# Block means of V from whole tiles, sums carried by transfers, and a new list of priorities in a three-layer kernel

## The chip, the cores and the metric

The kernel runs on one core of a Trainium2 chip. The metric is device time in microseconds (us) of one execution. The engines are TensorE (PE in the rows; PEld is its weight load), VectorE (DVE), ScalarE (ACT), GpSimd (POOL) and SyncE (SP), which issues all the transfers (DMAs).

## The reference, cut to what matters

Three layers run one after another on 2 sequences of 768 positions, all in float32.

1. Attention with 8 heads of 64. A position sees its neighbours within 15 positions, and also one summary of each of the 24 blocks of 32 positions: the key's summary is the maximum over the block, the value's summary is the mean.

```
k_sum = k.reshape(B, H, nb, block, D).max(axis=3)
v_sum = v.reshape(B, H, nb, block, D).mean(axis=3)
```

2. A mixture of four causal attention heads, gated by the best two of four logits, with projections `wq`, `wk`, `wv`, `wo`.
3. A channel mix: `r * (relu(xk @ w_k)**2 @ w_v)` with `r = sigmoid(xr @ w_r)`. Its three weight matrices come as float64 and are turned into float32 pairs on the chip.

## The kernel before, in words

The sequence is cut into 12 tiles of 128 positions (`t` = 0 to 5 for the first batch element, 6 to 11 for the second) for layer 1, and into 4 chunks of 384 for layers 2 and 3. Products that need full precision are split into a high and a low part and take three matmuls.

**Layer 1, per tile.** `stage1_scores` runs 32 small matmuls (L627) of queries against a key slab that holds a window of 96 keys and 24 block summaries. `stage1_softmax` adds the mask and takes the row maximum on DVE (L642, 8 per tile), the exponential with its row sum on ACT (L645, 8 per tile), one sum and one reciprocal for each half of the heads (L648, L650), and a multiplication by the reciprocal (L653 or L657). The probabilities lie in `pp` buffers, of which there are four, two per tile. `stage1_trans` transposes them on TensorE (L680) and copies them out, and `stage1_out` multiplies them by the values (L698). The value buffer of a half tile (`vw`; for some tiles it borrows `oh`, `ol`, `pq0` to `pq2`) holds 96 window rows loaded from memory and 24 rows of block means, which `put_val_sums` copies in from `vs`, two copies of 24x512 for each of the tiles 0 to 7, on whichever of DVE, ACT and POOL the planner chooses.

**Block means of V.** For batch element 0, `val_sums0` multiplies all 12 value windows, as they lie in `vw`, by a small matrix `own` that has a load of its own (L557, 4 matmuls per window), and copies the result to `vs`. It therefore needs every window of the first element. The rows of `vw` that hold no window are set to zero first (L493). For element 1, `sums1` loads V in four pieces of 96x8x128, folds each with three additions on DVE or POOL (L578), multiplies it by a selection matrix (L582) and copies it out on ACT (L584).

**Layers 2 and 3.** Projections of queries and keys (L770) and of values and gates (L788), scores (L870), transposes (L930), weighted values (L956), the output projection (L998); then L1106, L1129 and L1153 for the channel mix. Their weights pass through the two `stage` buffers and are split into high and low parts by copies and subtractions (L409, L411, L416, L418). The weights of layer 2 are loaded by `load_w12` after the first five tiles of layer 1 have been written down.

**What sets the order.** The program is not run in the order in which it is written. Each operation is handed to a planner (`Plan`) with an estimated cost, and some with several engines to choose from. The planner simulates the engines with fixed delays between them. It takes the ready operation that can start first, and among equals the one with the highest priority; priority is the length of the chain of work behind an operation, plus a bias. It does so 100 times with random numbers added to the priorities, keeps the shortest result (L193 to L213), and issues the instructions of every engine in that order. Each engine then works through its own list in order. Loads that are written down while `first[0]` is "sp" form a chain and keep their order on the SP queue.

Of the kernel before, what the change touches and what calls it, by code (L numbers as in the profile page):

```python
# [19 lines left out]
E = 4  # L20
# [6 lines left out]
NV = S // 8  # L27
# [30 lines left out]
ORDERS, SPREAD = 100, 1000.0  # L58
# [10 lines left out]
class Buf:  # L69


    def __init__(self, pool, shape, dt, name):
        self.pool, self.shape, self.dt, self.name = pool, shape, dt, name
        self.tile, self.slot, self.left, self.first, self.last = None, None, 0, None, 0.0
        self.hist = []
# [11 lines left out]
class Plan:  # L87
# [14 lines left out]
        "sp": dict(pe=995.0, act=995.0, dve=995.0, pool=995.0, sp=995.0),  # L102
    }
    HOLD = dict(pe=200.0, act=225.0, dve=200.0, pool=135.0, sp=995.0)
# [4 lines left out]
    for a in MODES:  # L109
        for b in MODES:  # L110
            SWITCH[a, b] = 92.0
# [48 lines left out]
    def run(self, alloc):  # L160
# [28 lines left out]
        need = {o: o.need for o in self.ops}  # L189
        left = {b: b.left for b in sum(self.order.values(), [])}  # L190
        best = None
        rng = random.Random(1)
        for n in range(ORDERS):  # L193
            for o in self.ops:
                o.need = need[o]
                o.rank = o.prio + (rng.random() * SPREAD if n else 0.0)
                o.eng, o.cost, o.fn, o.lock = o.ways[0]
            for b in left:
                b.left, b.slot, b.last = left[b], None, 0.0
            done = self.simulate()  # L200
            if done is None:
                continue
            end = max(o.end for o in done)
            if best is None or end < best[0]:
                best = (end, [(o, o.start, o.eng, o.cost, o.fn, o.end) for o in done], {b: b.slot for b in left})
        for b in left:
            b.slot = best[2][b]
        for o, o.start, o.eng, o.cost, o.fn, o.end in best[1]:
# [4 lines left out]
        return best[0]  # L213

    def simulate(self):
# [5 lines left out]
        cols = {}  # L221
# [27 lines left out]
        while len(done) < len(self.ops):  # L249
            best = None  # L250
            for e, cand in ready.items():
                mine = None
                for o in cand:
# [10 lines left out]
                    for b in o.bufs:  # L264
                        if b.slot is None:
# [5 lines left out]
                            t = max(t, sorted(free[b.pool])[n][0])  # L271
                    rank = o.rank
# [14 lines left out]
            for b in o.bufs:  # L287
                if b.slot is None:
                    free[b.pool].sort()
                    b.slot = free[b.pool].pop(0)[1]  # L290
                    nxt[b.pool] += 1
# [11 lines left out]
            if e == "sp":  # L303
                clock["sp"] = t + 560.0
                bus = max(bus, t + 1100.0) + o.cost
                o.end = bus
            for b in o.bufs:
# [41 lines left out]
def dma(nbytes, run=512):  # L349
    return nbytes / 275.0 * (1 if run >= 512 else 1.5 if run >= 384 else 2)  # L350
# [3 lines left out]
def attn_moe_rwkv(  # L354
# [15 lines left out]
    owns: bass.AP,  # L370
# [8 lines left out]
    NSM, NSE = 8, 4  # L379
# [18 lines left out]
    def load(dst, src, nbytes, run=512, w=None):  # L398
        op("sp", dma(nbytes, run), lambda: nc.sync.dma_start(dst(), src), w=w, stream=first[0])
# [52 lines left out]
    cst = buf("cst", [P, P + NB + 16])  # L452
    own = buf("x2", [P, 4 * NB - 4])
# [6 lines left out]
    sms, rss = buf("sms", [P, NSM, 4, 2]), buf("rss", [P, NSM, 4])  # L460
# [31 lines left out]
    for t in range(TPB):  # L492
        op("pool", 700, lambda t=t: nc.gpsimd.memset(vw[t][0].t[SROW[0]], 0.0), w=[(vw[t][0], "sum")])  # L493
# [8 lines left out]
    def slab(t):  # L502
# [3 lines left out]
        if b:  # L506
            load(lambda: k.t[:, :, NB:NB + SLAB], kS[b, :, :, tt * P:tt * P + SLAB], P * HP * SLAB * 4, 640,
# [15 lines left out]
    def load_v(t, s2):  # L523
# [3 lines left out]
        load(lambda: v.t[WROW[s2]], vp[b, a:a + KS0], KS0 * 2048, w=[(v, "win")])  # L527
# [17 lines left out]
    def val_sums0():  # L545

        vsm[0] = vs = buf("vs", [P, DM])
        p = bank("a2")
        for t in range(TPB):
            for s2 in range(2):  # L550
                v = vw[t][s2]

                def go(t=t, s2=s2, v=v):
                    n = NK if s2 == 0 else KS0
# [794 lines left out]
```

## Time and profile before

| | us |
|---|---|
| three runs | 1180.05, 368.61, 367.28 |
| median of them | 368.61 |
| the profiled execution | 368.59 |
| its span, first to last instruction | 366.8 |
| TensorE busy | 347.4 (95%) |
| VectorE busy | 256.1 (70%) |
| ScalarE busy | 219.7 (60%) |
| GpSimd busy | 75.5 (21%) |

The profiled execution agrees with the median; 1.8 us of it lie outside the span. The granted TensorE clock is full in all 40 slices of the span. Busy shares are means over the whole span, and a matmul counts as busy while it is in the pipeline, so that two that overlap, or one that waits within it, hide how much work there was. The transfers are dense in the first tenth and thin afterwards: the engines that move them are busy for 80 to 90% in the first slices and for a tenth or less in most of the last twenty.

### The profile page before, as it was taken

Reading aid. Unit: us, or ns where it says so; the run is one execution under the profiler, and the core shown is the slowest. Engines: PE = TensorE matmul, PEld = TensorE weight load, DVE = VectorE, ACT = ScalarE, POOL = GpSimd, SP = SyncE. Lnnn points to the kernel's source line nnn. Section 1 sums busy time; section 2 is a strip of 40 time slices with the busy share of each in tenths; the row PEclk is TensorE's granted clock in tenths of the full one; section 3 lists DMA queues with packets and bytes.
Section 4 is the critical chain, followed back from the end, with each engine's and each line's share of the span. In section 5 each row is a group of like instructions: output and inputs, shape, how many; then the busy total and the mean of one; then the engine's idle time right before and its main releaser. Section 6 shows DMA issues by size and latency. Waiting matters only on the chain.

```text
span 366.8 us, 7505 instructions
## 1 busy us (share of the span) xinstructions
PE 347.4 (95%) x2768; PEld 297.9 (81%) x2768; DVE 256.1 (70%) x813; ACT 219.7 (60%) x612; POOL 75.5 (21%) x105
## 2 busy tenths in 40 slices
PE   1687999999999999999999999999999999999996
PEld 0566988777877899797978798889988998889986
DVE  2899989899999867999999969219640576003511
ACT  2889757899979568898888766035610454015400
POOL 3228402315271003713414301000100001000000
PEclk9999999999999999999999999999999999999999
DMA  8996546753413310113334100100001000100001
GB/s 268 254 320 172 180 120 180 178 184 96 144 46 116 115 59 1 60 57 116 116 114 118 57 1 9 50 29 2 0 29 59 1 0 2 57 29 2 0 29 59
DMA packets 18740, 31.42 MB, mean 86 GB/s; under 512 B 1936, under 2 KB 9104, under 8 KB 18704
## 3 DMA queue, kind: packets, MB, share of 16 engines
q1 hardware_dynamic: 18704, 30.94, 27.3%
q8 instruction: 22, 0.36, 0.4%
q14 instruction: 14, 0.11, 0.1%
HBM read 27.79 MB, written 3.15 MB: 84 GB/s over the span
## 4 chain that ended last, share of the span: by engine, by line
PE 78%; DVE 13%; DMA 7%; issue 1%; SPq 0%
PE ps L1153 18%; PE ps L1129 16%; PE ps L1106 8%; PE ps L770 8%; PE ps L788 5%; PE ps L930 5%; PE ps L870 4%; PE ps L998 4%; PE a L956 3%; DMA qb<-in_qT 3%; PE a L698 2%; DVE pp L642 2%; DMA stage<-in_vp 2%; DMA vw<-in_vp 1%; PE ps L680 1%; PE ps L627 1%
## 5 line engine op out<-in xcount | busy, mean ns | idle before, releaser
L645 ACT ACTIVATE pp<-pp,nm 128x120 f32<-128x120 f32 x96 | 36.6, 386 | 6.2 <-DVE nm L642 6.1
L408 ACT ACTIVATE pp<-ps 128x512 f32<-128x512 f32 x12 | 7.1, 590 | 49.6 <-PE ps L1106 49.6
L890 ACT ACTIVATE pq<-pq,nm 128x128 f32<-128x128 f32 (+5 forms) x48 | 31.8, 663 | 7.9 <-DVE nm L877 5.2
L1159 DVE TENSOR_TENSOR wvgl<-ps,pp 128x512 f32<-128x512 f32 (+1 forms) x13 | 8.5, 650 | 40.0 <-PE ps L1153 40.0
L770 PE MATMUL ps<-x,wqkh 128*128 128x384 f32 x128 | 34.3, 349 | 0.5 <-DVE q L416 0.5
L877 DVE CUSTOM_DVE_ANT_0 pq<-ps,trm 128x384 f32<-128x384 f32 (+3 forms) x64 | 29.2, 502 | 4.0 <-PE ps L870 3.9
L1136 DVE SCALAR_TENSOR_TENSOR q<-ps,q 128x384 f32<-128x384 f32 x32 | 17.6, 554 | 18.3 <-ACT q L1135 17.9
L930 PE MATMUL ps<-cst,pq 128*128 128x128 f32 x168 | 25.0, 275 | 0.1
L642 DVE CUSTOM_DVE_ANT_0 pp<-ps,msk 128x120 f32<-128x120 f32 x96 | 22.3, 272 | 3.8 <-PE ps L627 3.7
L416 DVE TENSOR_TENSOR x<-q,x 128x384 fp32r<-128x384 f32 x24 | 13.2, 567 | 16.3 <-ACT x L408 16.1
L418 POOL TENSOR_TENSOR x<-q,x 128x384 fp32r<-128x384 f32 x8 | 12.0, 1498 | 61.2 <-ACT x L408 61.1
L1135 ACT ACTIVATE q<-ps 128x384 f32<-128x384 f32 x32 | 15.6, 489 | 13.9 <-PE ps L1129 12.7
L770 PEld LDWEIGHTS ps<-x,wqkh 128*128 128x128 f32 x128 | 22.1, 189 | 1.5 <-DVE q L416 0.7
L788 PE MATMUL ps<-wvgh,x 128*128 128x260 f32 x96 | 23.1, 304 | 0.0
L627 PE MATMUL ps<-kw,qb 64*64 64x120 f32 x320 | 12.0, 296 | 10.9 <-DMA qb<-in_qT 7.6
L1129 PE MATMUL ps<-x,wqkh 128*128 128x384 f32 x96 | 21.9, 341 | 0.0
L770 PE MATMUL ps<-x,wqkl 128*128 128x384 f32 x64 | 21.5, 337 | 0.0
L930 PEld LDWEIGHTS ps<-cst,pq 128*128 128x128 f32 x168 | 19.5, 141 | 1.8 <-issue 0.3
L956 PE MATMUL a<-th,vv 128*64 128x384 f32 (+2 forms) x144 | 20.7, 423 | 0.0
L408 ACT ACTIVATE th<-ps 128x384 f32<-128x384 f32 x45 | 19.6, 493 | 1.4 <-PE ps L930 1.3
L870 PE MATMUL ps<-ks,q 64*128 64x384 f32 (+3 forms) x192 | 20.3, 339 | 0.0
L1089 DVE SCALAR_TENSOR_TENSOR q<-x,mu,q 128x384 f32<-128x384 f32 x32 | 19.3, 612 | 0.8 <-ACT q L427 0.8
(229 smaller groups left out, 969.9 us busy)
## 6 DMA issues: line engine op xcount, KB each, us to landing
stage<-in_wk SPq DMA_DIRECT2D x8, 512.0 KB, 3.6
stage<-in_wv SPq DMA_DIRECT2D x8, 512.0 KB, 3.6
qb<-in_qT SPq DMA_DIRECT2D x12, 256.0 KB, 5.8
vw<-in_vp SPq DMA_DIRECT2D x16, 192.0 KB, 3.4
out_y<-wvgl SPq DMA_DIRECT2D x11, 256.0 KB, 2.0
stage<-in_wr SPq DMA_DIRECT2D x4, 512.0 KB, 4.0
kw<-in_kS SPq DMA_DIRECT2D x6, 320.0 KB, 3.6
ks<-in_kS SPq DMA_DIRECT2D x4, 400.0 KB, 5.1
```

The costliest lines, as they stand in the source:

```text
L642: op("dve", dve(NK), lambda i=i, p=p: nc.vector.tensor_tensor_reduce(pr.t[:, i], p.t[:, i * NK:(i + 1) * NK], msk.t[:, m], -0.125, BIG, AL ...
L645: op("act", act(NK, True) + 186, lambda i=i: nc.scalar.activation(pr.t[:, i], pr.t[:, i], AF.Exp, bias=nm.t[:, i:i + 1], scale=-1.0, accum ...
L770: mm(p.t[:, :C], a.t[:, kc, cols], x.t[:, kc, :], start=(kc == 0 and i == 0), stop=(kc == KC - 1 and i == 2))
L788: mm(p.t[:, :260], x.t[:, kc, tok], a.t[:, kc, :], start=(kc == 0 and i == 0), stop=(kc == KC - 1 and i == 2))
L870: mm(ps[e2].t[:, :z - a], q1.t[r, x, tok], ks.t[r, y, a:z], start=n == 0, stop=n == 2)
L877: nc.vector.tensor_tensor_reduce(pr.t[:, a:z], p.t[:, :z - a], trm.t[:, 512 - nk + a:512 - nk + z] if z == nk and not a else (trm.t[:, 512 ...
L890: nc.scalar.activation(pr.t[:, :nk], pr.t[:, :nk], AF.Exp, bias=nm.t[:, m:m + 1], scale=-1.0, accum_out=sme.t[:, k, i, 0:1]), r=[nm, (sme, ...
L930: lambda i=i, kb=kb, pr=pr: nc.tensor.transpose(p.t[:, i * P:(i + 1) * P], pr.t[:, kb * P:(kb + 1) * P], ident()),
L956: mm(acc.t[64 * e2:64 * e2 + 64, tq0 * P:(tq0 + cnt) * P], vv.t[:, kb, e * D:(e + 1) * D], th[e2].t[:, i0 * P:(i0 + cnt) * P], start=first ...
L1106: mm(p.t, a.t[:, kc, tok], w[2](), start=(kc == 0 and i == 0), stop=(kc == KC - 1 and i == 2))
L1129: mm(p.t[:, :C], w[2]()[:, mo:mo + P], a.t[:, kc, :], start=(kc == 0 and i == 0), stop=(kc == KC - 1 and i == 2))
L1153: mm(p.t[:, :n], a[2]()[:, tok], w[2]()[:, col], start=(m == 0 and i == 0), stop=(m == FC - 1 and i == 2))
```

## The change: what it does

- **Means of element 0.** V is loaded a second time, as two whole tiles of 128x3x512 (`val_tiles`, 768 KB each) in buffers of the pool `x`, in the chain ahead of the windows. The matrix `own` is now part of `consts`, and 24 matmuls replace 48. The zeroing of `vw` and the load of `own` go.
- **Means of element 1.** Three loads of 128x2x512 in `stage`, 24 matmuls into one bank, four copies out. The twelve additions go.
- **Carrying the means.** For every tile but the first, the two copies into `vw` become two transfers of 24x512 (48 KB) on the SP queue. For tile 0 one copy is on DVE and one on ACT by preference.
- **Probabilities of tiles 0, 1 and 2** lie in the three `x2` buffers, not in `pp`.
- **One sum and one reciprocal per tile** over 8 columns in place of two over 4.
- **Loads.** Weights for values and gates are loaded after the windows of tile 0, those for queries and keys after the windows of tile 2, the queries of tiles 2 and 3 after the windows of tiles 0 and 1.
- **Planner.** The 100 random orders go; 161 listed seeds (`STEPS`) each shift the priorities of some operations, all are applied, and one simulation gives the order. Delays and costs of transfers and of some matmuls change, and at most eight transfers are taken to be in flight.

```diff
-ORDERS, SPREAD = 100, 1000.0
+STEPS = (
+    785053421, 541001281, 764893564, 565041234, 822100463, 391705521, 731851593, 744830411, 695749570, 1026508739,
...
-        "sp": dict(pe=995.0, act=995.0, dve=995.0, pool=995.0, sp=995.0),
+        "sp": dict(pe=1150.0, act=1150.0, dve=1150.0, pool=1150.0, sp=1150.0),
...
+        for step in STEPS:
+            self.vary(step)
+        done = self.simulate()
...
+        width = rng.choice((20, 60, 200, 600))
+        a = rng.randrange(-width // 2, n)
+        share, size = rng.choice((0.05, 0.2, 0.6)), rng.choice((300.0, 1000.0, 3000.0, 8000.0))
+        for i in range(max(a, 0), min(a + width, n)):
+            if rng.random() < share:
+                self.ops[i].rank += rng.gauss(0.0, size)
...
+                flight.append(bus)
+                clock["sp"] = max(t + 480.0, flight[-8] + self.HOLD["sp"] if len(flight) > 7 else 0.0)
...
-    for t in range(TPB):
-        op("pool", 700, lambda t=t: nc.gpsimd.memset(vw[t][0].t[SROW[0]], 0.0), w=[(vw[t][0], "sum")])
...
+    def val_sums(b, vt, p, tiles):
+
+        def go(j, v):
+            for g in range(4):
+                mm(p.t[32 * g:32 * g + NB, 0:P], own(j), v()[:, g * P:(g + 1) * P], start=j == 0, stop=j == TPB - 1)
+
+        op("pe", 230 * len(tiles), lambda: [go(j, v) for j, v in tiles], r=[vt, cst], w=[p], stream="p1v",
+           mode="quarter")
...
+    def val_tiles(b, pl, n):
+
+        vt = []
+        for j in range(0, TPB, n):
+            v = buf(pl, [P, n, DM])
+            a = HALO + j * P
+            load(lambda v=v: v.t, vp[b, a:a + n * P].rearrange("(k p) n -> p k n", p=P), n * P * 2048, w=[v])
...
+            if t:
+                op("sp", dma(NB * 2048, 255.0), lambda v=v, s2=s2: nc.sync.dma_start(v.t[SROW[s2]], vsm[b].t[:NB]),
+                   r=[vsm[b]], w=[(v, "sum")])
...
-        prs = [buf("pp", [P, 4, NK]) for par in range(2)]
+        if t < 3:
+            both = buf("x2", [P, 2, 4, NK])
+            prs = [((both, par), lambda par=par: both.t[:, par]) for par in range(2)]
...
+        op("dve", 92, lambda: nc.vector.tensor_reduce(rss.t[:, k], sms.t[:, k], AX.X, ALU.add),
+           r=[(sms, (k, z)) for z in range(8)] + [(sms, "eps")], w=[(rss, k)])
...
+    vt0 = val_tiles(0, "x", 3)
...
     for t in range(TPB):
         for s2 in range(2):
             load_v(t, s2)
-        if t == 3:
-            load_q(2)
-    load_q(3)
+        if t < 2:
+            load_q(2 + t)
+        if t == 0:
+            load_wvg()
+        if t == 2:
+            load_wqk()
+            load(lambda: mu.t, mus, 4096, w=[mu])
+            load(lambda: trm.t, tri, P * 2048, w=[trm])
```

## Rows read from the trace of the kernel before

**Rows 1.** Windows: length, then busy us (count) by engine, clock, DMA share, GB/s.
```profile
0.00:19.60 19.60, 8.08 (x125) 6.13 (x126) 10.89 (x49) 11.01 (x46) 5.58 (x18) 1.00 0.90 259
19.60:38.40 18.80, 15.46 (x341) 12.65 (x341) 18.56 (x90) 17.17 (x69) 11.10 (x14) 1.00 0.85 253
62.90:75.10 12.20, 11.32 (x101) 9.24 (x102) 10.90 (x51) 10.25 (x45) 4.40 (x6) 1.00 0.70 187
75.10:207.50 132.40, 131.87 (x1157) 108.87 (x1157) 123.00 (x409) 111.21 (x294) 45.49 (x53) 1.00 0.30 95
207.50:366.80 159.30, 156.12 (x782) 139.16 (x782) 71.30 (x138) 54.27 (x108) 4.63 (x5) 1.00 0.06 20
```

**Rows 2.** Groups of TensorE instructions, 0 to 38.4 us: busy, mean ns, idle before, releaser.
```profile
L680 PE MATMUL ps<-cst,pp 128*120 128x128 f32 x37 | 6.1, 284 | 1.7 <-DVE pp L653 1.3 <-DVE rss L648 0.2
L627 PE MATMUL ps<-kw,qb 64*64 64x120 f32 x128 | 6.0, 339 | 10.9 <-DMA qb<-in_qT 7.6 <-ACT kw L408 3.3
...
L627 PE MATMUL ps<-f,qb 64*64 64x120 f32 x64 | 2.1, 268 | 0.4 <-DMA qb<-in_qT 0.2
L557 PE MATMUL a<-vw,x 120*24 120x128 f32 (+1 forms) x32 | 1.8, 409 | 0.0
L557 PE MATMUL a<-pq,x 120*24 120x128 f32 (+1 forms) x48 | 1.7, 275 | 0.0
```

**Rows 3.** Chain that ended last, in order of time: start, length, what; the paces.
```profile
39.04 1.81 PE ps L788 x15
...
42.48 0.44 PE ps L680 x4
...
78.54 1.08 PE a L698 x32
...
87.43 0.98 PE ps L627 x32
```

**Rows 4.** TensorE in order of time, 21 to 30 us: start, length, instruction.
```profile
21.95 0.86 PE L557 MATMUL a<-pq,x 96*24 96x128 f32 x24
...
25.36 0.34 PE L698 MATMUL a<-q,vw 120*64 120x64 f32 x4 [0.37 <-DVE vw L409]
...
29.52 0.69 PE L698 MATMUL a<-q,vw 120*64 120x64 f32 x16 [1.06 <-DVE x L416]
```

**Rows 5.** The same chain as in Rows 3, its start.
```profile
1.63 5.88 DMA qb<-in_qT
7.52 5.48 DMA vw<-in_vp
13.02 6.44 DMA qb<-in_qT
```

**Rows 6.** VectorE's copies out of `vs`: count, least, median and largest ns, first and last start.
```profile
L409 DVE COPY vw<-vs x1: 416/416/416, 24.9 to 24.9; 24x512 f32<-24x512 f32 x1
L409 DVE COPY oh<-vs x1: 715/715/715, 26.6 to 26.6; 24x512 f32<-24x512 f32 x1
L409 DVE COPY ol<-vs x1: 745/745/745, 27.3 to 27.3; 24x512 f32<-24x512 f32 x1
L409 DVE COPY pq<-vs x1: 385/385/385, 35.1 to 35.1; 24x512 f32<-24x512 f32 x1
```

**Rows 7.** VectorE's sums and reciprocals of the softmax, 0 to 38.4 us.
```profile
L650 DVE RECIPROCAL rss<-rss 128x4 f32<-128x4 f32 x10 | 1.7, 170 | 0.0
L648 DVE TENSOR_REDUCE rss<-sms 128x4 f32<-128x8 f32 x10 | 1.5, 155 | 0.9 <-ACT pp L645 0.8
```

**Rows 8.** The same chain as in Rows 3, 63 to 76 us.
```profile
63.73 6.76 DMA stage<-in_vp
...
72.66 1.45 DVE stage L578
...
75.11 0.74 PE ps L582 x4
```

**Rows 9.** SP queue in order of time: start, time to issue, transfer.
```profile
20.74 0.39 SPq L399 DMA_DIRECT2D stage<-in_wvg  x1
...
34.58 0.39 SPq L399 DMA_DIRECT2D stage<-in_wqk  x1
```

**Rows 10.** Transfers by tile: engine, count, KB each, median us from issue to landing.
```profile
x<-in_owns SPq DMA_DIRECT2D x1, 46.0 KB, 6.9
```

More of the change, by code (lines that the diff above doesn't have):

```diff
@@ L73, in __init__ @@
         self.pool, self.shape, self.dt, self.name = pool, shape, dt, name
-        self.tile, self.slot, self.left, self.first, self.last = None, None, 0, None, 0.0
+        self.tile, self.slot, self.left, self.first, self.last, self.open = None, None, 0, None, 0.0, 0.0
         self.hist = []
@@ L188, in run @@
             o.prio += far + o.cost
[L189 to L208, printed above, removed]
+        for o in self.ops:
+            o.rank = o.prio
+            o.eng, o.cost, o.fn, o.lock = o.ways[0]
+        for step in STEPS:
+            self.vary(step)
+        done = self.simulate()
+        assert done is not None, "no operation can be placed"
+        for o in done:
             for b in o.bufs:
@@ L543, in put_key_sums, with val_sums_out @@
             rnd("act", lambda o=o: k.t[:, :, o:o + NB], lambda: ksm[b].t, HP * NB, [ksm[b]], [(k, ("sums", e))], True)
[L545 to L554, printed above, removed]
-                    o = s2 * (2 * NB - 2) + 2 * (NB // 2 - 1 - (2 * t + s2))
-                    for g in range(4):
-                        mm(p.t[32 * g:32 * g + NB, 0:P], own.t[:n, o:o + NB], v.t[:n, g * P:(g + 1) * P],
-                           start=t + s2 == 0, stop=t + s2 == TPB)
-                op("pe", 230, go, r=[own, (v, "win")] + ([(v, "sum")] if s2 == 0 else []), w=[p], stream="p1v",
-                   mode="quarter")
+    def val_sums(b, vt, p, tiles):
[4 more added lines that the diff above has]
+           mode="quarter")
+    def val_sums_out(b, p):
+        vs = vsm[b]
         for g in range(4):
@@ L662, in stage1_trans @@
     def stage1_trans(t, par, state):
-        pr = state[t, par]
+        pk, pr = state[t, par]
+        pk = [(pk[0], (pk[1], i)) for i in range(4)] if t < 3 else [pk] * 4
         p = bank("ps")
@@ L963, in go @@
                         fn()
-                op("pe", sum(18.0 + 1.9 * r[6] * P for r in runs), go,
+                op("pe", 58.0 + 1.677 * P * sum(r[6] for r in runs), go,
                    r=sum((ths[gi] for gi in some), []) + [(vv, r[4]) for r in runs], w=[acc], stream="p2a", mode="half")
@@ L1218, in attn_moe_rwkv @@
     stage1(1, c1)
-    first[0] = "sp"
-    load_w12()
-    first[0] = None
+    load_wo()
     sums1()
```

180 lines of the change are left out of this document (91 added, 89 removed), and 16 rows, old and new, of the table STEPS.

## The prediction

> **What bounds the kernel now.** I read the windows first [rows 1]. From 75.1 us to the end TensorE is busy all but 0.5 us of one stretch and 3.2 us of the other, at full clock. Before 38.4 us it is not, and it stands still for 0.9 us between 62.9 and 75.1. VectorE, the other candidate, is busy for 18.56 of 18.80 us between 19.6 and 38.4, and only there does it leave TensorE short. So the question is what the change does to the first 38 us and to the stretch around 70 us; elsewhere, work that leaves VectorE, ScalarE or GpSimd is cover and no gain.
>
> Busy time overstates TensorE's work, because a matmul in the pipeline counts even where it waits. I therefore price the matmuls of the first 38.4 us [rows 2] at the pace at which the chain passes runs of them [rows 3, 4]: 192 of L627 at 0.98/32, 5.9 us; 37 of L680 at 0.44/4, 4.1; four tiles of L698 at 1.08, 4.3; 96 of L557 (12 windows of 8; 80 of them shown) at 0.86/24, 3.4; twelve of L788 at 1.81/15, 1.4. That is 19.1 us of work in 38.4 us: **19.3 us are lost**. The waits name 10.9 of these: 7.6 for the first queries and 3.3 for the second half of the first key slab [rows 2]. No line of the change makes the first queries come sooner, so some 11.7 us could be won here at the very most.
>
> The chain shows why the rest is lost [rows 5]: first queries, then a window of values, then the queries of tile 2, each issued only when the one before it had landed, until 19.5 us. From there VectorE carries the chain. The means of the values come last: the last L557 starts at 21.95 us, and the first product with the values at 25.36 us, after a copy of the means [rows 4].
>
> **The change, part by part.** The sum is made against the profiled execution, 368.59 us, which is 0.02 us below the median of the runs.
>
> *Removed from VectorE in the first stretch.* Its four copies out of the means take 0.42 + 0.72 + 0.75 + 0.39 = 2.3 us [rows 6]; the one at 24.9 us is tile 0's, of whose two copies VectorE keeps one by preference, so 1.85 us go. Of ten sums and ten reciprocals five each go [rows 7], 5 x (0.155 + 0.170) = 1.6 us by their busy time, about half of it in sequence, since neighbours on VectorE overlap: 0.8 us. Together 2.65 us, bounds 1.85 and 3.5. The price of the merge is that the first half's probabilities wait for the second half's four exponentials; VectorE has other rows to do meanwhile, and if it did not, the wait would be that of ScalarE for four, and the gain of 0.8 us would be gone.
>
> *Moved loads.* By issue order, what had landed when tile 2's queries came at 19.46 us was 1.64 MB of keys, three tiles of queries at 0.26, masks and constants 0.32 and twelve windows at 0.197: 5.1 MB, which the 259 GB/s of the stretch [rows 1] make 19.7 us. In the new order the whole tiles (1.57 MB) and two windows (0.39 MB) stand there in place of twelve windows: 4.7 MB, 18.0 us. Tile 2's queries come 1.7 us sooner, and the tiles that the means need land after 4.0 MB, 15.5 us, in place of 22. So the first product with the values can start some 5 us earlier than 25.36 us, and does not bound any more; VectorE does. In all 1.57 MB more are moved, 6.1 us of transfers at 259 GB/s; they push back the windows of tiles 3 to 5, which are not used before tile 3's product. I take 1.7 us of gain, bounds 0 (VectorE is busy anyway) and 5.
>
> These two together: **-4.35 us**, bounds 0 and -8.5. The x2 buffers let tiles 0 to 2 hold their probabilities while the means are awaited; that wait is now short, so I give them nothing of their own. The zeroing ran on GpSimd while it had nothing else: nothing. 48 fewer L557 matmuls are 1.7 us of TensorE, in the stretch where it is short of work: nothing.
>
> *Around 70 us.* The chain waits 6.76 us for a load of V, and from its landing at 70.49 to the selection matmul at 75.11 another 4.6 us pass with the additions on VectorE [rows 8]. The change puts the matmuls directly behind the landing. TensorE fills most of this from other work and stands still for 0.9 us only [rows 1]; between 0.9 and 4.6 the nearer row is the idle time, and I take **-1.4 us**, bounds 0 and -4.6.
>
> *The new matmuls of the means of element 1.* 48 records at 0.86/24 are 1.7 us on TensorE where it is full. They replace 8 of L582, priced by the four that took 0.74 us [rows 8], so 1.5 us. Three separate visits may each break a run of other matmuls: **+0.4 us**, bounds 0 and +1.2.
>
> *The transfers that carry the means.* Fourteen of 48 KB. The nearest row in size is the load of `own`, 46 KB, which landed 6.9 us after issue among the bulk loads [rows 10]; a copy took 0.4 to 0.75 us. Before, 4.2 us lay between the first two products with the values [rows 4]. With means ready near 18 us, a carry of 6.9 us ends at 25, before the 29.5 at which tile 1's product ran: hidden by that, price 0; if the cover is gone, up to 2.7 us (6.9 less 4.2), which I keep for the range. Of such transfers the Trainium skill (DMA: Bandwidth & Descriptors, Rules for kernel authors) says that below 64 KB one pays mostly overhead and should merge them; it speaks against this part of the change. The load of 46 KB agrees in that it was no quicker than those of several hundred. By that rule as a bound on the path the sum would be 2.7 us worse.
>
> *The new order.* The program is placed anew, and the trace of before cannot show how. A better order can only pay where TensorE is short: of the 19.3 us, after the 7.6 us wait and the 4.35 already booked, 7.3 are left, most in the first stretch. A worse one has the 3.3 us wait [rows 2] as its nearest row. I take **-3 us**, nearer the middle than either end because half of what is left is softmax that must precede the first products; bounds -7.3 and +3.3.
>
> Sum: 368.59 - 4.35 - 1.4 + 0.4 - 3.0 = **360.2, say 360 us**.
>
> **The rivals.**
>
> *A: the order closes most of the gaps.* All of the 7.3 us and the 4.6 us around 70 us go: 368.6 - 4.35 - 4.6 + 0.4 - 7.3 = 353 us. For it: the second half of the queries-and-keys weights, issued at 34.58 us, 13.8 us after the first load of weights [rows 9], is now in the chain before the windows of tile 3, so that projections could fill TensorE from 30 us. Against it: VectorE has 18.56 us of work in that stretch and loses only 2.65.
>
> *B: what is removed is cover.* VectorE's list shortens, but 1.57 MB more delay what it waits for, and TensorE becomes full at the same 38 us; around 70 us the 0.9 us go. 368.6 - 0.9 + 0.4 = 368 us. For it: the transfers are busy for 85 to 90% of the first two stretches [rows 1]. Against it: the extra megabytes come ahead of loads that are used last.
>
> *C, slower: the SP queue stands at the weights.* The second piece of the queries-and-keys weights needs a `stage` buffer that the values-and-gates weights leave only when they have been split. Before, 13.8 us passed between these two issues [rows 9], with nothing urgent behind them. Now the windows of tiles 3 to 5 and the transfers of the means can stand behind that wait. The first load of weights is issued near 16 us; if the wait is again 13.8 us, it ends at 30, and means and windows land up to 6.9 us later, at 37 us. Tile 1's product, at 29.5 us before, would then run at 37: +7.4 us, and the gains of the first stretch are gone: 368.6 + 7.4 - 1.4 + 0.4 = 375 us. It decides from the point at which that wait ends after 23 us, when a carry no longer lands by 29.5. Against it: GpSimd, which did the splitting, has 5.58 us of work in the first 19.6 [rows 1] and can do it at once.
>
> **How the numbers follow.** The forecast has 0.58, A 0.17, B 0.18, C 0.07. The time is the forecast's, 360. Its own range is 355 to 365 (first stretch 2 us, order 3 us, to either side). The range reaches to just below A and just into B: 351 to 368, leaving out C and the edges of A and B. About 2% is what a measurement of this kernel can tell from no change: 361.2 and 376 us. Two thirds of the forecast's case lie below 361.2, with A 0.39 + 0.17 = 0.56; the rest of it with B and half of C makes 0.37 for no change; 0.07 remain for slower, half of C and a badly placed order.
>
> **What would show it.** Right: the last means matmul before 18 us, the first L698 near 20, a stretch of lost TensorE time that ends near 33 us, no VectorE work between the landing of element 1's V and its matmuls, and TensorE full behind that. Wrong: SP waiting for a splitting of weights while L698 waits for a transfer of the means (C); TensorE still short of work at 38 us with VectorE full (B); or a gain that lies behind 75 us, where I see nothing to win.

## The result, and the profile after

The changed kernel takes 364.49 us (median of four, 362.83 to 364.86) beside 368.69 us for the kernel before on the same chip: **a ratio of 0.9893, 95% interval 0.9865 to 0.9921**, 1.1% or some 4 us faster. The forecast was 360 us, 2.3% faster. The sign was right; of the 8.35 us that the sum foresaw, half came. The profiled execution took 364.77 us, its span is 362.9 us against 366.8: the two traces differ by 3.9 us, nearly as much as the medians (4.2).

The head of the profile page: busy time, share of the span, instructions, for each engine.

```profile
PE 345.3 (95%) x2760; PEld 298.7 (82%) x2760; DVE 253.5 (70%) x793; ACT 215.3 (59%) x607; POOL 56.8 (16%) x83
```

The five stretches of [rows 1], the last one shorter by the gain (length, then busy time and count of PE, PEld, DVE, ACT, POOL, the granted clock, the DMA share, GB/s):

```profile
0.00:19.60 19.60, 9.00 (x141) 6.95 (x145) 10.62 (x46) 11.45 (x46) 3.97 (x14) 1.00 0.93 291
19.60:38.40 18.80, 16.34 (x302) 13.89 (x294) 15.32 (x71) 14.38 (x53) 4.95 (x6) 1.00 0.90 241
62.90:75.10 12.20, 11.55 (x143) 8.54 (x132) 11.94 (x64) 11.26 (x53) 1.01 (x1) 1.00 0.76 241
75.10:207.50 132.40, 132.17 (x1164) 111.76 (x1161) 125.14 (x397) 107.79 (x284) 35.08 (x47) 1.00 0.28 90
207.50:362.90 155.40, 152.32 (x764) 135.59 (x762) 70.32 (x136) 50.82 (x101) 8.54 (x8) 1.00 0.06 21
```

VectorE, full between 19.6 and 38.4 us before, now stands still for 3.5 of 18.8 us there. TensorE is only 0.9 us busier (16.34 against 15.46). VectorE was relieved, and then something else came last. TensorE in order of time shows what (start, length, instruction, and in brackets how long the engine was idle before it and what ended that):

```profile
13.22 1.50 PE L566 MATMUL a<-x,cst 128*24 128x128 f32 x24
15.78 1.49 PE L566 MATMUL a<-x,cst 128*24 128x128 f32 x24 [1.06 <-DMA x<-in_vp]
...
20.01 1.15 PE L727 MATMUL a<-q,vw 120*64 120x64 f32 x32
...
23.46 1.05 PE L648 MATMUL ps<-f,qb 64*64 64x120 f32 x32 [1.27 <-DMA qb<-in_qT]
...
26.69 1.28 PE L727 MATMUL a<-q,vw 120*64 120x64 f32 x32
...
36.31 2.07 PE L648 MATMUL ps<-kw,qb 64*64 64x120 f32 x64 [0.45 <-DMA qb<-in_qT]
```

The matmuls of the means are done at 17.3 us and the first product with the values starts at 20.0, 5.3 us sooner than in [rows 4]. But the scores of tiles 4 and 5, which the kernel before ran at 27.41 and at 34.54 us, now run together at 36.31, when their queries land:

```profile
27.41 1.05 PE L627 MATMUL ps<-kw,qb 64*64 64x120 f32 x32
...
34.54 1.05 PE L627 MATMUL ps<-kw,qb 64*64 64x120 f32 x32
```

The chain that ended last goes through these loads (after; start, length, what):

```profile
5.13 7.38 DMA x<-in_vp
...
12.53 10.80 DMA qb<-in_qT
...
24.93 4.62 DMA stage<-in_wqk
...
30.08 6.19 DMA qb<-in_qT
```

In place of VectorE, which carried the chain from 19.5 us before, stand the second read of V, the queries of tile 3, a piece of weights, and the queries of tiles 4 and 5. The queue of SP shows how they got so late (after; start, time to issue, transfer):

```profile
18.55 0.92 SPq L602 DMA_DIRECT2D vw<-vs  x1
19.85 0.77 SPq L602 DMA_DIRECT2D ol<-vs  x1
21.37 0.71 SPq L602 DMA_DIRECT2D vw<-vs  x1
22.31 1.74 SPq L602 DMA_DIRECT2D pq<-vs  x2
24.10 0.71 SPq L602 DMA_DIRECT2D oh<-vs  x1
24.93 1.26 SPq L419 DMA_DIRECT2D stage<-in_wqk  x1
...
27.21 2.77 SPq L419 DMA_DIRECT2D pq<-in_vp  x6
30.08 0.88 SPq L419 DMA_DIRECT2D qb<-in_qT  x2
```

Before, the queries of tiles 3 to 5 were issued one after the other from 16.82 us on, the last of them at 18.5 us:

```profile
16.82 1.99 SPq L399 DMA_DIRECT2D qb<-in_qT  x3
```

**How much TensorE did by 38.4 us**, at the paces of [rows 3, 4] that the prediction used. The groups of after up to 38.4 us (out, in, shapes, count, busy us, mean ns, idle before):

```profile
L648 PE MATMUL ps<-kw,qb 64*64 64x120 f32 x128 | 5.8, 339 | 10.0 <-ACT kw L428 9.5 <-DMA qb<-in_qT 0.5
L820 PE MATMUL ps<-wvgh,x 128*128 128x260 f32 x23 | 5.7, 314 | 0.7 <-DVE x L436 0.7
L709 PE MATMUL ps<-cst,x 128*120 128x128 f32 x24 | 4.1, 326 | 0.0
L820 PE MATMUL ps<-wvgl,x 128*128 128x260 f32 x11 | 3.1, 282 | 0.0
L566 PE MATMUL a<-x,cst 128*24 128x128 f32 x48 | 3.0, 419 | 1.1 <-DMA x<-in_vp 1.1
L727 PE MATMUL a<-q,vw 120*64 120x64 f32 x64 | 2.4, 226 | 0.1
L648 PE MATMUL ps<-f,qb 64*64 64x120 f32 x64 | 2.1, 268 | 1.3 <-DMA qb<-in_qT 1.3
L727 PE MATMUL a<-pt,pq 120*64 120x64 f32 x32 | 1.2, 225 | 0.0
L709 PE MATMUL ps<-cst,pp 128*120 128x128 f32 x8 | 1.1, 279 | 0.0
L727 PE MATMUL a<-pt,oh 120*64 120x64 f32 x16 | 1.0, 228 | 0.0
L727 PE MATMUL a<-pt,ol 120*64 120x64 f32 x16 | 1.0, 222 | 0.0
```

192 scores make 5.9 us, 32 transposes 3.5, four tiles of products 4.3, 34 of the value projection 4.1 and 48 means 1.7: 19.5 us, and **18.9 us are lost, against 19.3 before**. Without the means it is 17.8 us of work against 15.7, a lead of 2.1 us; 1.7 of it are the 48 matmuls that the means no longer take. What the change was to win in this stretch, lost time, hardly moved.

Around 70 us V lands almost when it did, at 69.9 us, and its means follow at once, not at 75.11 as in [rows 8] (the chain again):

```profile
69.95 0.64 PE ps L566 x16
```

TensorE stands still for 0.65 us of this stretch in place of 0.88. The row of long series with which the kernel closes begins 3.4 us sooner, and takes 0.5 us less to the end of the span (its first series, before, then after):

```profile
220.69 16.75 PE ps L1153 x72
```

```profile
217.25 16.72 PE ps L1185 x72
```

Of these 3.4 us some 2 were there at 38.4 us. Counted in the same way at 80 us the lead is still 2.0 us, so the rest arose behind that.

### The profile page after: what moved, and what is told of

Read it like the earlier page. It is cut to its first block, busy times and chain, and to the rows that moved or that the text cites. A ratio compares the mean times of both kernels' runs of the same rounds, so it can differ in the third digit from the quotient of the medians.

```text
span 362.9 us, 7455 instructions
## 1 busy us (share of the span) xinstructions
PE 345.3 (95%) x2760; PEld 298.7 (82%) x2760; DVE 253.5 (70%) x793; ACT 215.3 (59%) x607; POOL 56.8 (16%) x83
## 4 chain that ended last, share of the span: by engine, by line
PE 81%; DMA 11%; DVE 4%; ACT 2%; SPq 1%; issue 0%; ACTq 0%
PE ps L1161 19%; PE ps L1185 18%; PE ps L1138 9%; PE ps L802 7%; PE a L988 5%; PE ps L962 5%; DMA qb<-in_qT 5%; PE ps L902 5%; PE ps L1030 4%; PE ps L820 3%; PE a L727 2%; DMA x<-in_vp 2%; PE ps L648 2%; DMA stage<-in_vp 2%; PE ps L709 1%; DMA stage<-in_wqk 1%
## 5 line engine op out<-in xcount | busy, mean ns | idle before, releaser
L428 ACT ACTIVATE pp<-ps 128x512 f32<-128x512 f32 x10 | 5.9, 593 | 50.6 <-PE ps L1138 50.6
L1168 DVE SCALAR_TENSOR_TENSOR q<-ps,q 128x384 f32<-128x384 f32 x32 | 17.3, 554 | 17.5 <-ACT q L1167 17.2
L669 ACT ACTIVATE pp<-pp,nm 128x120 f32<-128x120 f32 x72 | 27.5, 384 | 2.5 <-DVE nm L666 2.3
L1167 ACT ACTIVATE q<-ps 128x384 f32<-128x384 f32 x32 | 15.6, 488 | 13.8 <-PE ps L1161 12.8
L820 PE MATMUL ps<-wvgh,x 128*128 128x260 f32 x96 | 22.3, 302 | 0.7 <-DVE x L436 0.7
L802 PE MATMUL ps<-x,wqkl 128*128 128x384 f32 x64 | 21.6, 337 | 0.0
L962 PEld LDWEIGHTS ps<-cst,pq 128*128 128x128 f32 x168 | 19.6, 140 | 2.1 <-issue 0.5
L1161 PE MATMUL ps<-x,wqkl 128*128 128x384 f32 x96 | 19.5, 338 | 0.0
L648 PEld LDWEIGHTS ps<-kw,qb 64*64 64x64 f32 x320 | 9.7, 150 | 11.5 <-ACT kw L428 9.9
L1185 PE MATMUL ps<-ks,pq 128*128 128x512 f32 (+1 forms) x78 | 19.0, 378 | 0.0
L428 ACT ACTIVATE th<-ps 128x384 f32<-128x384 f32 x42 | 18.7, 487 | 0.2
```

Source lines behind the costliest of these rows:

```text
L648: mm(ps[par].t[c, i * NK:(i + 1) * NK], q.t[r, i, c], k.t[r, i, o:o + NK], start=True, stop=True)
L669: op("act", act(NK, True) + 186, lambda i=i, z=z, pr=pr, nm=nm: nc.scalar.activation(pr()[:, i], pr()[:, i], AF.Exp, bias=nm.t[:, i:i + 1] ...
L802: mm(p.t[:, :C], a.t[:, kc, cols], x.t[:, kc, :], start=(kc == 0 and i == 0), stop=(kc == KC - 1 and i == 2))
L820: mm(p.t[:, :260], x.t[:, kc, tok], a.t[:, kc, :], start=(kc == 0 and i == 0), stop=(kc == KC - 1 and i == 2))
L962: lambda i=i, kb=kb, pr=pr: nc.tensor.transpose(p.t[:, i * P:(i + 1) * P], pr.t[:, kb * P:(kb + 1) * P], ident()),
L1161: mm(p.t[:, :C], w[2]()[:, mo:mo + P], a.t[:, kc, :], start=(kc == 0 and i == 0), stop=(kc == KC - 1 and i == 2))
```

## The experiments

Ratios are to the kernel before, run beside it on the same chip, with 95% intervals. "Lists as they are" means that every engine keeps its order of instructions, so that nothing moves but what is told.

**What is the order, what the work?** The change's program, first without its list of shifts, then with before's search of 100 random orders; and before's own program with another random seed.

```diff
-STEPS = (785053421, 541001281, ... 161 numbers)
+STEPS = ()                      # no_steps
+ORDERS, SPREAD = 100, 1000.0    # search100: the loop of before over the new program
-        rng = random.Random(1)
+        rng = random.Random(2)  # seed2, in the kernel before
```

> The changed kernel without the list of 161 shifts: the same work, loads and planner costs, priorities by chain length alone, one simulation. Theory (the gain behind 80 us is the order's): without the shifts the kernel gives back what it wins there and more, ratio to the kernel before 0.995 to 1.01 (366 to 372 us). Rival (the removed work carries the gain, the order adds little): ratio 0.987 to 0.993.

> The changed kernel's work, loads and planner costs, but its order found as in the kernel before: the shortest of 100 simulations with random numbers added to the priorities. Compared with the kernel before, the way of finding an order is the same and the work differs. Theory (the work alone is worth 1 to 2 us, the order the rest of the 4): ratio 0.993 to 0.998. Rival (the work carries all): 0.987 to 0.991. If above 1, the new work and loads cost time unless the order is fitted to them.

> The kernel before with another seed for its 100 random orders, nothing else. It shows what a mere re-placing of the same work is worth. If orders found in this way are alike, 367.5 to 369.5 us, and the 4 us of the change come from its work and loads; if they differ by 2 us or more, the order alone can make or hide an effect of that size.

Measured: no_steps 1.0171 (1.0135 to 1.0206), search100 **0.9998 (0.9974 to 1.0022)**, seed2 1.0007 (0.9987 to 1.0027). In the one order that before's way finds for it the new work is worth nothing, and the same program moves by 2.8% with its order alone (the order includes the choice of engine where an operation can go to several). A part of this is TensorE's clock: the mean granted clock is 0.986 to 0.991 in the four executions of no_steps, 0.990 to 0.995 in eight of the ten of search100, and 1.00 in all four of the changed kernel. What a lower clock costs is shown in the last section.

**Does VectorE's work bound the first stretch?** Once by adding to the changed kernel (two sums and reciprocals of four columns in place of one of eight, 24 instructions more), once by taking from the kernel before what the change takes.

```diff
-nc.vector.tensor_reduce(rss.t[:, k], sms.t[:, k], AX.X, ALU.add)
+[nc.vector.tensor_reduce(rss.t[:, k, a:a + 4], sms.t[:, k, a:a + 4], AX.X, ALU.add) for a in (0, 4)]   # split
...
-        op("dve", 85, lambda: nc.vector.tensor_reduce(...        # less_work, kernel before
+        op("dve", 85, lambda: None if par else nc.vector.tensor_reduce(...
+        ... the reciprocal alike; copies of the means of t > 0: lambda: None
```

> The changed kernel with every engine's list as it is, but each tile's sum and reciprocal over 8 columns are done as two over 4, 24 small instructions more on VectorE at the same places. By the rows of before they cost 0.07 to 0.17 us each, 0.16 us in sequence for a pair, 1.9 us of VectorE in all, most of it where TensorE is full. Theory (cover): not more than 0.3 us slower than the changed kernel, ratio 0.989 to 0.991. Rival (VectorE bounds wherever it is busy): 1 to 2 us slower, ratio 0.992 to 0.995.

> The kernel before with its lists of instructions as they were, less what the change takes from the engines: the copies of the block means into the value buffers of all tiles but the first (14) and one of the two sums and reciprocals of each tile (24 instructions of VectorE) are left out. The second half's probabilities are scaled by the first half's reciprocals and the rows of the means are zero in all tiles but the first, so layer 1 computes other numbers; products also wait for no means. The prediction gave this work 2.65 us (bounds 1.85 to 3.5) in the first 38 us: about 365.8 us, ratio 0.990 to 0.995. The theory that VectorE's small work is cover, and that what comes last there is a load or the chain of the softmax: at most 1 us, ratio 0.997 to 1.000.

Measured: split 0.9899 (0.9878 to 0.992), as the changed kernel; less_work **0.9965 (0.9947 to 0.9983)**, 1.3 us. Less work in VectorE's full stretch is worth half of the 2.65 us that the prediction gave it. The run takes out more than VectorE's part, since some of the 14 copies were on ScalarE and GpSimd and the products no longer wait for any of them; against that, GpSimd sets five more blocks of `vw` to zero. VectorE is still full there (30 to 40 us, columns as in [rows 1]: less_work, then the kernel before):

```profile
30.00:40.00 10.00, 9.46 (x159) 8.50 (x161) 9.97 (x45) 8.93 (x39) 4.76 (x6) 1.00 0.71 212
```

```profile
30.00:40.00 10.00, 8.77 (x158) 7.78 (x155) 10.00 (x49) 9.38 (x38) 7.54 (x9) 1.00 0.73 206
```

**What do 1.57 MB cost?** Added to the kernel before behind the last window of values; taken, to a third, from the changed kernel and from search100.

```diff
+            if t == 5 and s2 == 1:      # more_bytes: behind this load, into tiles nobody reads
+                for i in range(2):
...
+                    nc.sync.dma_start(d, vp[0, c:c + 3 * P].rearrange("(k p) n -> p k n", p=P))
...
-            load(lambda v=v: v.t, vp[b, a:a + n * P]...          # third_v, search_third, b == 0
+            nc.sync.dma_start(v.t[:, 0], vp[0, a:a + P])
```

> The kernel before with every list of instructions as it was, and two whole tiles of V (768 KB each, the change's own second read) loaded into tiles that nobody reads, on the SP queue between the last window of values and the queries of tile 3. So this is the change's 1.57 MB alone, in the order of before. The prediction priced these bytes at nothing, because what they push back is not used before tile 3's product: 368.4 us, ratio 0.997 to 1.003. The theory that the bytes cost what they delay (queries of tiles 3 to 5 and the first weights come up to 6 us later, while TensorE is short of work): the scores of tile 3 start near 28 us in place of 22.95, and the kernel is 2 to 4 us slower, ratio 1.005 to 1.011.

> The changed kernel with every engine's list as it is, but of each of the two whole tiles of V of element 0 only the first third is loaded and used three times; the block means of element 0 are wrong by this. 1.05 MB fewer are moved in the first 20 us, about 4 us at 259 GB/s. Theory (the first stretch is bound by the bytes ahead of the queries): everything behind comes 3 to 4 us sooner, VectorE's idle time at 30 to 40 us moves forward or shrinks, and the kernel takes 361 to 363 us. Rival (bytes don't bound; the order of the lists does): 364 to 365 us.

> The changed kernel's work and loads in the order that before's search of 100 random orders gives (as in the run search100, 0.9998 of before), and of each whole tile of the first element's V only the first 128 rows are loaded and used three times: 0.52 MB in place of 1.57, the means of that element are wrong. If the bytes of the second read are what ate the gain of the removed work, 1.5 to 2.5 us come back here as they did in the changed kernel's own order (third_v): 0.993 to 0.996 of before. If the work is worth nothing and the bytes too, it stays at 0.998 to 1.002.

Measured: more_bytes **1.0105 (1.0075 to 1.0135)**, 3.9 us slower; third_v 0.9847 (0.982 to 0.9875), some 1.7 us faster than the changed kernel for 1.05 MB, with intervals that just overlap; search_third 0.9995 (0.998 to 1.001), no different from search100. In more_bytes TensorE waits for the queries of tile 3 and then runs near the lower of its two clock levels, 1.2 GHz or 0.5 of full speed (TensorE in order of time, then two windows):

```profile
26.32 1.81 PE L636 MATMUL ps<-f,qb 64*64 64x120 f32 x32 [4.08 <-DMA qb<-in_qT]
```

```profile
26.00:28.00 2.00, 1.68 (x32) 1.47 (x32) 0.00 (x0) 0.00 (x0) 0.35 (x1) 0.61 1.07 365
28.00:30.00 2.00, 1.91 (x18) 1.25 (x16) 1.84 (x11) 1.40 (x4) 0.04 (x1) 0.54 1.07 385
```

VectorE does nothing between 26 and 28 us: it is the queries that are missing. The 3.9 us hold both the wait and the slower stretch behind it. The price of the bytes is real, but it is that of what stands behind them in the list at hand. In third_v no load is left in the chain between 12 and 36 us, and TensorE is busy for all of the 10 us from 30 (first row third_v, then the changed kernel):

```profile
30.00:40.00 10.00, 10.00 (x154) 9.43 (x149) 6.91 (x45) 7.16 (x30) 0.29 (x1) 1.00 0.98 262
```

```profile
30.00:40.00 10.00, 9.55 (x166) 8.60 (x167) 6.63 (x35) 6.39 (x22) 0.82 (x2) 1.00 0.96 273
```

That row proves no gain by itself: split shows the same 10.00 us of TensorE at an unchanged time. And VectorE is hardly fuller with two thirds of the bytes gone (6.91 against 6.63 us).

Search_third shows why the same bytes can be worth nothing. In search100 TensorE waits 2.20 us for the queries of tile 3 at 22.34 us; in search_third they are there and the scores run at 21.15. But the product of tile 2 starts at 29.54 us in the one and at 29.47 in the other, after a gap in which the profile shows nothing that TensorE waited for. Behind the gap the granted clock is 0.51 from 30 to 32 us (search_third; in search100 it is 0.50 from 32 to 34):

```profile
29.47 0.34 PE L714 MATMUL a<-pt,oh 120*64 120x64 f32 x4 [2.16 <-issue]
```

**Queries sooner.** In the changed kernel with its lists as they are, loads are moved on the SP queue alone.

```diff
+        moved = [o for o in done if o.mark in late]     # late: ("q", 4), ("q", 5) or ("q", 3)
+        done = [o for o in done if o not in moved]
+        i = next(i for i, o in enumerate(done) if o.mark == at) + 1
+        done[i:i] = moved    # q_first: q4, q5 behind tile 2's windows; q3_first: q3 behind q2; both_first: both
```

> The changed kernel with every engine's list as it is, but on the SP queue the loads of the queries of tiles 4 and 5 stand right behind the windows of tile 2, ahead of the weights for queries and keys and of the transfers of the means (in the changed kernel tile 4's are issued at 30.08 us and its scores start at 36.31). Theory (loads starve VectorE): VectorE is idle for 3.4 of 10 us between 30 and 40 us only because these queries come late; scores of tile 4 start before 31 us, that idle time goes, and the kernel takes 361.5 to 363.5 us against 364.5. Rival (TensorE has projections meanwhile, so the late queries cost nothing): 364 to 365 us, or up to 1 us slower because the weights and means land 2 us later.

> The changed kernel with every engine's list as it is, but on the SP queue tile 3's queries stand ahead of the weights for values and gates and of the windows of tile 1 (0.92 MB fewer before them, 3.5 us at 259 GB/s). TensorE waits 1.3 us for them at 23.46 us, and in the runs with other SP orders up to 2.5 us with the clock at half afterwards. Theory (bytes ahead of the queries are what costs): the wait goes, 0.5 to 1.5 us faster than the changed kernel, ratio 0.985 to 0.988. Rival (something else then waits for the weights, which land 1 us later): ratio 0.989 to 0.991.

> The changed kernel with its lists as they are, but on the SP queue the queries of tile 3 stand right behind those of tile 2 and the queries of tiles 4 and 5 right behind the windows of tile 2. The two runs that did one of these each came to 0.9871 and 0.9876 of before, the changed kernel to 0.9893. If each saves a wait of its own, about 0.986 of before (363 us); if the queue only exchanges one late load for another, it stays at 0.988 to 0.990.

Measured: q_first 0.9871 (0.9844 to 0.9898), q3_first 0.9876 (0.9851 to 0.99), both_first 0.9885 (0.9855 to 0.9915); none can be told from the changed kernel's 0.9893. In q_first the queries of tiles 4 and 5 no longer come last, but their scores stay in their place in TensorE's list and run at 36.06 us. Before that, TensorE waits 2.46 us for the queries of tile 3 and then runs at a granted clock of 0.53 from 22 to 24 us and 0.62 from 24 to 26:

```profile
22.50 1.88 PE L655 MATMUL ps<-f,qb 64*64 64x120 f32 x32 [2.46 <-DMA qb<-in_qT]
...
36.06 1.87 PE L655 MATMUL ps<-kw,qb 64*64 64x120 f32 x64
```

In both_first the queries of tiles 4 and 5 are issued from 15.85 us on and their scores run at 34.42, with no wait in front of them: what they stand behind there is TensorE's own list. VectorE is busy for 7.29 us of the ten from 30 on, against 6.63 in the changed kernel, 6.92 in q_first and 6.91 in third_v. So the theory that VectorE is idle there only because these queries, or the bytes ahead of them, come late has fallen for these lists: the place of the scores in TensorE's list keeps VectorE waiting also when both are out of the way.

In q3_first most of the wait for queries goes, and the projection of the values waits instead for what VectorE copies out of the first tiles (waits of TensorE to 45 us), again with a granted clock of 0.50 behind it, from 26 to 28 us. One late thing is exchanged for another.

```profile
PE ps L827 <- DVE x L434: 2.0, 1, 2.0
```

**The transfers of the means.** As copies on GpSimd; then as transfers on a queue that GpSimd issues, alone and with the queries moved as in both_first.

```diff
-nc.sync.dma_start(v.t[SROW[s2]], vsm[b].t[:NB])
+nc.gpsimd.tensor_scalar(v.t[SROW[s2]], vsm[b].t[:NB], 1.0, 0.0, ALU.mult, ALU.add)   # copies
+nc.gpsimd.dma_start(v.t[SROW[s2]], vsm[b].t[:NB])                                   # pool_queue, pool_queue_q
```

> The changed kernel with every engine's list as it is, but the 14 transfers that carry the means are 14 copies on GpSimd at the same places of the program. Theory (the SP queue is held up by them): SP is free of some 8 us of issuing between 18 and 36 us, the queries of tiles 4 and 5 are issued about 5 us sooner, and the kernel takes 361 to 363.5 us. First rival (carrying by transfers is free): 364 to 365 us. Second rival (GpSimd's copies get in VectorE's way or come too late): 365 to 367 us.

> The changed kernel with its lists as they are, but the 14 transfers that carry the means are issued by GpSimd on a queue of its own and not by SP. In the changed kernel ten of them are issued between 18.6 and 35.5 us, 0.7 to 0.9 us of SP each, and the chain goes through SP there: tile 3's queries land at 23.34 us and only then SP goes on, queries of tiles 4 and 5 are issued at 30.08. If the prediction's zero for the transfers is right, nothing changes: 0.987 to 0.991 of before. If they cost what they hold back on SP, the queries of tiles 4 and 5 are issued 2 to 4 us sooner and the kernel comes to 0.980 to 0.986; the second load of queries-and-keys weights, which waits for a buffer until 24.9 us, bounds that gain.

> As pool_queue, and on the SP queue the queries of tile 3 stand right behind those of tile 2 and the queries of tiles 4 and 5 right behind the windows of tile 2, ahead of the queries-and-keys weights. If SP's queue is what makes the first 40 us long, this takes both holds away and is the fastest of all, 0.978 to 0.984 of before (360 to 362 us). If the bytes in flight bound the loads and not the queue, one load is only exchanged for another: 0.986 to 0.990, as in both_first (0.9885).

Measured: copies 0.9937 (0.9913 to 0.9962), pool_queue 0.9912 (0.988 to 0.9944), pool_queue_q 0.992 (0.9902 to 0.9938). None of the gains that SP's queue was to give came. Transfers are no worse than copies, and SP's time for them bounds nothing: once they are off the queue, SP stands at the next thing, the buffer of the queries-and-keys weights (waits of SP's queue, 10 to 40 us, pool_queue: total, times, longest):

```profile
SPq L419 <- DVE wvgl L436: 5.1, 1, 5.1
```

and the queries of tile 5 land at 36.06 us (36.27 in the changed kernel); the scores of tile 4 run 1.5 us sooner, at 34.82 (its chain):

```profile
29.66 6.40 DMA qb<-in_qT
```

**Equal effort for either work.** The program of before and that of the change, both with the changed kernel's planner, each with two lists of shifts of its own, found by some 10,000 random trials of `vary` that were kept when the planner's own simulation got shorter.

```diff
-STEPS = (785053421, 541001281, ... 161 numbers)
+STEPS = (506927179, 796816699, ... 20 to 35 numbers)   # new_work_*, and with before's operations old_work_*
```

> Before's work and loads as they were (means of the values from the windows, copies, two sums per tile), placed by the changed kernel's planner with its costs, and with listed shifts of priorities found for this program: some 10,000 random shifts were tried and 30 kept. So this is the change's way of finding an order, without its work. If the order carries the change (the rest came to 0.9998 of before), 0.987 to 0.993. If the order needs the new work to be worth anything, 0.996 to 1.003.

> As old_work_1 with another set of shifts, found from another start (35 kept): how far two orders of the same work lie apart. Within 0.5% of old_work_1 if the search decides, further if each order has its own luck.

> The change's work and loads with listed shifts found in the same way and with as many trials as in old_work_1 (20 kept). The prediction's sum makes this 5.35 us faster than old_work_1 (4.35 + 1.4 - 0.4), 1.5% of before; if work and loads are worth nothing in themselves, the two differ by less than 0.5%.

> As new_work_1 with another set of shifts (25 kept). With both pairs the work's own value is the difference of the two means: 1.5% by the prediction's sum, within 0.5% of zero if the order is all.

Measured: old work 1.0069 (1.0043 to 1.0096) and 0.9989 (0.9973 to 1.0005); new work 0.9964 (0.9945 to 0.9983) and 0.9956 (0.9937 to 0.9974). The means differ by 0.7%, some 2.5 us. That is no more than the 0.8% between the two orders of the old work, so with two orders of each it is likely, but not shown, that the new work wins: the better list of the old work and the two of the new lie 0.3% apart, with intervals that overlap slightly. By these means the new work wins about half of the 5.35 us that the prediction's sum would have here, and it depends on the order whether any of it shows (nothing in search100). The theory that the order alone carries the change fell in this form: this way of finding an order brings the old work nothing. Nor does it bring the new work what the 161 shifts do: 0.996 against 0.9893.

VectorE from 30 to 40 us tells the two works apart in every order (new_work_1, then old_work_2):

```profile
30.00:40.00 10.00, 8.43 (x160) 7.69 (x155) 4.82 (x21) 4.72 (x13) 0.61 (x3) 1.00 0.93 241
```

```profile
30.00:40.00 10.00, 8.69 (x158) 7.27 (x154) 9.96 (x48) 9.78 (x41) 7.25 (x11) 1.00 0.50 143
```

Half empty in one, full in the other, and TensorE equally busy in both: the transfers are dense (0.93) where VectorE is empty. In the six kernels with the old loads VectorE is busy for 9.9 to 10.0 us of these ten, in the fourteen with the new ones for 4.1 to 7.3. Less_work is one of the six (9.97): the removed work is not what empties VectorE there; that comes with the new loads and the lists made for them.

## Why the prediction was right and wrong

**The step that failed is the first-stretch term, -4.35 us**, both halves of it. It was to come out of the 19.3 us that TensorE loses before 38.4 us, and only 0.4 of these went (18.9 are lost after).

*Work removed from VectorE, -2.65.* Taken out of the kernel before, with the copies on the other engines and the waits for them, it is worth 1.3 us (less_work), below the term's own lower bound of 1.85. VectorE was full there and stayed so (9.97 of 10 us); an instruction of a full engine shortens the kernel only if TensorE waits next for the work behind it. The term also halved the sums and reciprocals because neighbours overlap; in the trace of before a sum at 19.55 us, its reciprocal and the next instruction start 0.20 and 0.21 us apart and do not overlap, so that at their full length the term would have been larger, and further off.

*Moved loads, -1.7, with 1.57 MB at nothing.* The prediction said that these "push back the windows of tiles 3 to 5, which are not used before tile 3's product". It overlooked that the queries of tiles 4 and 5 stand behind them as well. They were issued by 18.5 us before and at 30.1 after, and their scores, at 27.41 and 34.54 before, ran at 36.31. Not the bytes alone do this: ahead of these queries on SP's queue now also stand transfers of the means, a piece of weights issued at 24.93 us and six windows, and when the queries were moved ahead of these, the scores kept their late place in TensorE's list (both_first). That the bytes cost something is shown in before's lists (3.9 us, with the clock that fell) and likely in the change's (1.7 for two thirds of them). What the term said of the early part came true: the scores of tile 2 ran at 19.03 us without a wait for their queries, and the first product at 20.01.

Together, the new work and loads were to bring 5.35 us, with the two terms around 70 us. In before's search they brought 0.0 (0.9998), in the pairs of equal effort about 2.5, which is not clear of the spread between orders. **Rival B** comes nearest for this stretch: VectorE's list became shorter, and TensorE is filled no sooner than before. But its reason, 1.57 MB that delay what VectorE waits for, is only a part of it: VectorE stays as idle with two thirds of them gone (third_v). And its time of 368 us lacked the order's gain. Rival A, an order that closes most of the gaps, did not come: 18.9 us stay lost.

*Around 70 us, -1.4.* The matmuls did follow the landing at once, but TensorE's idle time fell by 0.2 us, not 1.4. The 0.9 us that TensorE stood still before were the most that could be won, and the term took more: the additions lay beside other matmuls.

*Means of element 1, +0.4.* Three visits of 16 matmuls at 0.64 us (the last one's length, above) are 1.9 us for 1.5, as priced; what the visits cost the whole was not tried alone.

*Fewer matmuls of the means of element 0, priced at nothing.* Lost time up to 38.4 us stayed (18.9 against 19.3), so the 1.7 us of matmuls that went appear as lead. That is an account; it was not tried alone.

*Transfers, at nothing.* Right: off SP's queue they bring nothing, and as copies the kernel is some 1.6 us slower, with intervals that just overlap. In pool_queue they took 4.2 to 7.3 us from issue to landing, near the price of 6.9, and the cover held (tile 1's product ran at 26.69). The Trainium skill (DMA: Bandwidth & Descriptors, Rules for kernel authors) says that below 64 KB a transfer pays mostly overhead, and that many of them should be merged. This case agrees in that 48 KB were no quicker to land than the 256 KB of the three loads at 16.82 us before, which took 5.7 to 6.0; what part of this is overhead, and whether merging helps, no run here shows.

*The new order, -3.0.* From search100 to the changed kernel, the same work in another order, it is 1.05%, 3.9 us: near in size, wrong in place, and so near by luck. A part of it is the clock, which did not fall in the changed kernel. Counted as above, search100 is some 2 us behind the changed kernel at 80 us, so that half of the 3.9 arose behind that, where the prediction saw "nothing to win" because TensorE is busy there. The likely reason, which no run shows, is that a matmul that waits within the pipeline counts as busy too. How the 161 shifts were found, and what in this order does it, stays open; the searches here did not reach it. The buffers `x2` and the earlier weights, which the prediction gave nothing, were not tried alone.

*Rival C* had its condition: the second piece of weights was issued at 24.93 us, after the 23 at which it was to decide, and 15.6 us after the first load of weights, which came at 9.29 us and not near 16. Its price did not come, since the transfers of tile 1 stand ahead of that wait; what does stand behind it are windows and the queries of tiles 4 and 5.

*The chances.* The prediction adds 0.19, B's 0.18 and half of C's 0.07 to 0.37; they make 0.41.

## What to carry to other kernels

When a change adds bytes, write down every load that stands behind them in the queue with the time at which its first reader runs; the price is that of the first late one, and it is another in every order. Work that is taken from an engine which is full for 20 us does not shorten the kernel by its own length: take it out alone and see (here half of it came back). And before a change that comes with a new order is called good, run its work in the old way of ordering: here that separated a gain of 1.1% from one of nothing.

## What the runs showed of the hardware

- After a stretch without work TensorE ran at the lower of its two clocks (1.2 GHz, 0.5 of full speed). In more_bytes it did nothing from 22.2 to 26.3 us; the granted clock was then 0.61 and 0.54 in two windows of 2 us, and 32 score matmuls took 1.81 us in place of the 1.05 that they take in the changed kernel at 23.46. A late load is paid twice. After the wait of 2.46 us in q_first they took 1.88. The changed kernel's own wait of 1.27 us at 23.46 cost no clock, nor did the 2.20 us in search100 (1.00 from 22 to 26 us).
- The same program falls to the lower clock in some executions and not in others. Of search_third's twelve, three have a mean granted clock of 1.00 and took 366.5 to 367.1 us; nine have 0.994 or 0.995 and took 367.7 to 369.0. Between the medians lie 1.4 us, a third of what the whole change brought.
- A transfer of 48 KB from one tile to another takes SP 0.71 to 0.92 us to issue, and GpSimd 0.51 to 0.74 in pool_queue. The first 512 KB of the queries-and-keys weights took SP 0.38 us, the second 1.26, so that the size does not set it (the transfers from `vs` to `pq` in the changed kernel: count; least, median and largest ns; first and last start):

```profile
L602 SPq DMA_DIRECT2D pq<-vs x6: 713/722/760, 22.3 to 34.8; - x6
```
